# Keys of a local attention in one ring of blocks, and a stored order of instructions in place of a planner

## The chip, the cores and the metric

The kernel runs on one core of a Trainium2 chip. The metric is the time of one execution on the device in microseconds (us); the median of three runs of the kernel before is 1020.16 us (1020.14 to 1020.78). The engines are named as in the profile: PE (TensorE, with PEld for its weight loads), DVE (VectorE), ACT (ScalarE), POOL (GpSimd), and SP, the queue that issues every DMA here. Each engine is given its instructions in a fixed order, and they wait on semaphores of the other engines.

## The reference

Causal attention with a window of 64 positions over 4 batches, 8 heads, 576 positions and 64 channels, then two gated layers over the 2304 tokens (512 to 1536 to 512 channels):

```python
mask = (rel >= 0) & (rel < 64)
attn = softmax(where(mask, scale * q @ k.T, -1e9)); x = attn @ v
xn = x / sqrt(mean(x * x) + 1e-06) * rms_g
x = (silu(xn @ w_gate) * (xn @ w_val)) @ w_out          # first layer
x = (sigmoid(x @ w2_gate) * (x @ w2_val)) @ w2_out      # second layer
```

## The kernel before, in words

**Attention.** The work unit is 64 query positions of one batch with all heads; a batch has 9 units, 36 in all. Queries and keys are loaded in tiles of 128 positions, that is two units; the last tile of a batch holds one. With a window of 64, unit i needs the keys of its own 64 positions and of the 64 before. `st_s` computes its scores: four head pairs, for each a product of 128 query rows (two heads) with 128 keys in f32. In an odd unit both key blocks lie in one tile, and L387 is one matmul of 128 columns. In an even unit (other than the first of a batch) the blocks lie in two tiles, and L389 and L390 are two matmuls of 64 columns each. Keys lie in two buffers `kt` by turns, and the third tile of the program in a place of its own (`kt2`). The mask is added by a matmul (L383) in the first two blocks of tokens, and by DVE (L399) in the others; then follow the row maximum (L396 or L400), four exponentials on ACT (L403), and the division (L404 to L406). `st_tr` transposes on PE (L419), `st_pv` multiplies with the values (L455).

**The layers.** Tokens go in six blocks of 384. Float32 weights and activations are carried as pairs of f16 numbers, high and low part, and each product is three f16 matmuls. A gate or value product for 128 of the 1536 channels is twelve matmuls into one PSUM bank of two (`gv`, L551); there are 288 such products. ACT reads a gate product (L563), and then DVE reads it in the gate step L565 (first layer); DVE's L576 or L578 reads the value product. The bank is free for the next product only then. L592 to L597 split the result, and L611 to L613 (first layer) or L617 to L619 (second) multiply with the output weights.

**The weights** arrive in float64 bit patterns in 1 MB pieces, and `w_max` (L220), `w_conv` (L244 to L256) and `w_split` (L302 to L315) turn them into f16 pairs on DVE and ACT. This takes place beside attention, mostly in the first half of the program.

**The order.** The program is traced once. `arrange` then groups the instructions (a run of matmuls into one bank counts as one), gives each a length by the rules in `price`, finds from the tiles they touch which must wait for which, and lays them on the engines by eight rounds of list scheduling forward and backward. The best of these rounds gives the order on every engine, which is pinned with dependences that cost no semaphore.

## Time and profile before

| | us |
|---|---|
| median of three runs | 1020.16 |
| the profiled execution | 1016.32 |
| its span, first to last instruction | 1014.5 |
| PE busy in it | 959.0 |
| DVE busy in it | 584.4 |
| ACT busy in it | 409.7 |

The profile shows one execution, the profiled one; the runs took somewhat longer than it. A matmul in f32 appears as two records. Busy times of an engine are unions: what overlaps counts once. The end of a matmul in the profile is modelled, so what a group takes is best read from the start of one group to the start of the next.

### The profile page before, as it was taken

What the parts mean: (1) busy time and instruction counts of PE and PEld (TensorE: products, weight loads), DVE (VectorE), ACT (ScalarE), POOL (GpSimd) and SP (SyncE); (2) the same over time, 40 slices, a digit from 0 to 9 for tenths busy, and PEclk for the clock granted to TensorE, in tenths of its full rate; (3) what the DMA queues carried; (4) which work ended last, traced back from release to release, by engine and by line L of the source; (5) the groups of instructions that cost most, each with busy time, mean ns of one, the idle gap of its engine ahead of it and who ended that gap; (6) DMA issues with size and microseconds to landing.
All of it is one profiled execution on the core that took longest, in us unless ns stands there. A gap on an engine that the chain in (4) does not pass through costs nothing.

```text
span 1014.5 us, 14919 instructions
## 1 busy us (share of the span) xinstructions
PE 959.0 (95%) x6176; PEld 583.0 (57%) x6176; DVE 584.4 (58%) x1124; ACT 409.7 (40%) x787; POOL 34.9 (3%) x40
## 2 busy tenths in 40 slices
PE   6667899789999999999999999999999999999998
PEld 6535666456655675675555555555555555555554
DVE  6989998998778888978838813212222222222221
ACT  5478867567342446344414312222222222122122
POOL 0110000100010001001001000000000000000000
PEclk9789999999999999999999999999999999999999
DMA  8455345041530220220013000000000000000000
GB/s 294 122 178 166 116 126 177 11 162 31 197 120 1 52 85 21 95 94 12 1 42 115 12 1 1 1 1 32 1 32 1 1 32 1 1 32 1 1 32 31
DMA packets 43187, 61.54 MB, mean 61 GB/s; under 512 B 23408, under 2 KB 31984, under 8 KB 38640
## 3 DMA queue, kind: packets, MB, share of 16 engines
q1 hardware_dynamic: 43120, 60.60, 18.4%
q8 instruction: 48, 0.79, 0.3%
q14 instruction: 19, 0.16, 0.1%
HBM read 55.87 MB, written 4.72 MB: 60 GB/s over the span
## 4 chain that ended last, share of the span: by engine, by line
PE 80%; DVE 14%; ACT 4%; issue 1%; POOL 0%; DMA 0%; SPq 0%; ACTq 0%; POOLq 0%
PE gv L551 47%; PE o L619 5%; PE o L618 5%; PE o L617 5%; PE o L611 4%; PE o L612 4%; PE o L613 4%; PE at L455 1%; DVE wmax L220 1%; DVE wl L256 1%; DVE th L565 1%; DVE wl L315 1%; PE at L390 1%; PE at L419 1%; PE at L387 1%
## 5 line engine op out<-in xcount | busy, mean ns | idle before, releaser
L551 PE MATMUL gv<-xhl,wl 128*128 128x384 f16 x3456 | 600.8, 329 | 31.4 <-DVE th L565 27.7
L551 PEld LDWEIGHTS <-wl 128*128 128x128 f16 x3456 | 338.6, 98 | 268.3 <-issue 45.5
L597 DVE SCALAR_TENSOR_TENSOR hh<-th,hs,hh 128x384 f16<-128x384 f32 x72 | 44.5, 618 | 238.4 <-ACT hh L596 238.4
L596 ACT ACTIVATE hh<-th,hs 128x384 f16<-128x384 f32 x72 | 44.4, 616 | 256.0 <-PE o L618 243.5
L619 PE MATMUL o<-wl,hh 128*128 128x512 f16 x216 | 81.9, 379 | 0.0
L617 PE MATMUL o<-wl,hh 128*128 128x512 f16 x216 | 81.9, 379 | 0.0
L618 PE MATMUL o<-wl,hh 128*128 128x512 f16 x216 | 81.9, 379 | 0.0
L254 ACT ACTIVATE wl<-wl 128x1024 uint16<-128x1024 uint32 (+1 forms) x32 | 78.8, 2470 | 5.4 <-DVE wl L249 5.3
L578 DVE SCALAR_TENSOR_TENSOR th<-th,gv 128x384 f32<-128x384 f32 x72 | 39.9, 554 | 68.0 <-PE gv L551 68.0
L592 ACT ACTIVATE hh<-th 128x384 f16<-128x384 f32 x48 | 25.1, 523 | 122.8 <-PE o L613 101.4
L563 ACT ACTIVATE th<-gv,tg 128x384 f32<-128x384 f32 x72 | 41.8, 581 | 57.0 <-DVE hh L593 26.3
L611 PE MATMUL o<-hh,wl 128*128 128x384 f16 x192 | 62.8, 327 | 0.0
L612 PE MATMUL o<-hh,wl 128*128 128x384 f16 x192 | 62.7, 327 | 0.0
L613 PE MATMUL o<-hh,wl 128*128 128x384 f16 x192 | 62.6, 326 | 0.0
L563 ACT ACTIVATE th<-gv,be 128x384 f32<-128x384 f32 x72 | 41.8, 580 | 48.9 <-DVE hh L597 43.2
L565 DVE SCALAR_TENSOR_TENSOR th<-th,gv 128x384 f32<-128x384 f32 x72 | 39.7, 551 | 16.9 <-ACT th L563 15.9
L593 DVE TENSOR_TENSOR hh<-th,hh 128x384 f16<-128x384 f32 x48 | 29.6, 617 | 33.0 <-ACT hh L592 32.4
L403 ACT ACTIVATE sm<-sm,nm 128x128 f32<-128x128 f32 x96 | 37.4, 391 | 17.6 <-DVE nm L400 17.5
L220 DVE TENSOR_REDUCE wmax<-wl 128x1 f32<-128x1024 f32 (+1 forms) x37 | 43.5, 1182 | 1.7 <-DMA wl<-in_moe_w_val_dram 1.7
L576 DVE SCALAR_TENSOR_TENSOR th<-th,gv 128x384 f32<-128x384 f32 x72 | 39.4, 547 | 8.2 <-PE gv L551 7.9
L613 PEld LDWEIGHTS <-wl 128*128 128x128 f16 x288 | 28.2, 98 | 18.8 <-issue 0.2
L611 PEld LDWEIGHTS <-wl 128*128 128x128 f16 x288 | 28.3, 98 | 18.3 <-issue 0.2
(168 smaller groups left out, 1040.5 us busy)
## 6 DMA issues: line engine op xcount, KB each, us to landing
wl<-in_moe_w_gate_dram SPq DMA_DIRECT2D x12, 1024.0 KB, 4.8
wl<-in_moe_w_val_dram SPq DMA_DIRECT2D x12, 1024.0 KB, 5.4
wl<-in_moe_w_out_dram SPq DMA_DIRECT2D x11, 1024.0 KB, 4.9
vn<-in_v_dram SPq DMA_DIRECT2D x28, 256.0 KB, 2.8
kt<-in_k_dram SPq DMA_DIRECT2D x15, 256.0 KB, 3.7
qbd<-in_q_dram SPq DMA_DIRECT2D x30, 128.0 KB, 3.7
out_dram<-vn SPq DMA_DIRECT2D x12, 256.0 KB, 2.0
out_dram<-sm SPq DMA_DIRECT2D x6, 256.0 KB, 2.0
```

What stands on the lines that cost most here:

```text
L220: V.tensor_reduce(out=r1[:, i:i + 1], in_=wraw(layer, j + i)[:, :, 1].bitcast(F32), axis=AX.X, op=ALU.max, apply_absolute_value=True)
L254: A.activation(out=r, in_=lo, func=AF.Copy, scale=2.0 ** -29)
L551: T.matmul(pb[:, 0:n], lhsT=w_, rhs=x_, start=(c == 0), stop=(c == m - 1))
L563: A.activation(out=th[:, 0:n], in_=pg[:, 0:n], func=AF.Tanh, scale=sc)
L565: V.scalar_tensor_tensor(out=th[:, 0:n], in0=th[:, 0:n], scalar=1.0, in1=pg[:, 0:n], op0=ALU.add, op1=ALU.mult)
L597: V.scalar_tensor_tensor(out=h[:, 1, 0:n], in0=th[:, 0:n], scalar=sc, in1=h[:, 0, 0:n], op0=ALU.mult, op1=ALU.subtract)
L611: T.matmul(o[c][:, 0:n], lhsT=wh[:, cs], rhs=hi, start=st, stop=False)
L612: T.matmul(o[c][:, 0:n], lhsT=wh[:, cs], rhs=lo, start=False, stop=False)
L613: T.matmul(o[c][:, 0:n], lhsT=wl[:, cs], rhs=hi, start=False, stop=en)
L617: T.matmul(o[t], lhsT=h[:, 0, ts_], rhs=wh, start=st, stop=False)
L618: T.matmul(o[t], lhsT=h[:, 0, ts_], rhs=wl, start=False, stop=False)
L619: T.matmul(o[t], lhsT=h[:, 1, ts_], rhs=wh, start=False, stop=en)
```

## The change

**The ring.** Keys now lie in one tile `kring` of 16 blocks of 64 keys: two slots of eight blocks, and in a slot two blocks (first and second half of the tile) for each head pair. A block of one slot and one of the other, for the same pair, are a constant step apart, so the two operands of an even unit become one operand with a step, and L389 and L390 become one matmul of 128 columns. Where the newer tile is in the first slot, the blocks come in swapped order (`swapped`): the mask is then a rolled one and the values are loaded in two halves of 64 rows, exchanged. The two units that touch the third tile of the program stay as they were. In the first unit of a batch, DVE's mask and maximum and the exponentials take 64 columns instead of 128, and a memset fills the rest (only in the blocks without the mask matmul).

```diff
+    kring = cst.tile([P, 4 * NP, 64], F32, name="kring")
+    def kslot(ti):
+        return (ti - (ti > 2)) % 2
+    def whole(ti):
+        return ti not in (2, 3)
+    def swapped(u):
+        b, i = units[u]
+        ti = b * TPB + i // 2
+        return i % 2 == 0 and i > 0 and whole(ti) and kslot(ti) == 0
...
-        a = kt2 if ti == 2 else ap_.tile([P, NP, P], F32, tag="kt", name="kt", bufs=2)
+        a = kt2 if ti == 2 else kring[:, 2 * NP * kslot(ti):2 * NP * kslot(ti) + 2 * NP, :].rearrange("p (c h) x -> p c (h x)", c=NP)
...
+            elif whole(ti):
+                x = 2 * c if swapped(u) else 2 * c + 1
+                y = 2 * NP + (2 * c + 1 if swapped(u) else 2 * c)
+                T.matmul(pb[:, c * P:(c + 1) * P], lhsT=lhsT, rhs=kring[:, x:y + 1:y - x, :], start=first, stop=first or c == NP - 1)
             else:
                 T.matmul(pb[:, c * P:c * P + 64], lhsT=lhsT, rhs=kt[ti - 1][:, c, 64:128], start=first, stop=first)
                 T.matmul(pb[:, c * P + 64:(c + 1) * P], lhsT=lhsT, rhs=kt[ti][:, c, 0:64], start=first, stop=first or c == NP - 1)
...
+        if swapped(u):
+            SY.dma_start(out=a[0:64], in_=v[b, s0 + 64:s0 + 128, :])
+            SY.dma_start(out=a[64:128], in_=v[b, s0:s0 + 64, :])
...
+            m = 1 if i == 0 or swapped(u) else 0
+            w = 64 if i == 0 else P
+            if i == 0:
+                V.memset(s[:, :, 64:P], 0.0)
+            V.scalar_tensor_tensor(out=s[:, :, 0:w], in0=pv[:, :, 0:w], scalar=scale, in1=masks[:, m:m + 1, 0:w].to_broadcast([P, NP, w]), op0=ALU.mult, op1=ALU.min)
```

**The order.** `spans`, `price` and the scheduling in `arrange` are gone. `arrange` still groups the instructions, and then unpacks a stored table of positions, one for each group, and pins that order. The table is for all five engines.

```diff
+ORDER = (
+    'c-nPV31CxIy1xIp*-n!*P1>XzO<P*pri@w&QkJ&Eq81dGVNhTY@gd8DhbWe1a48IkqF}|cID@Y+BPjdGC{F|jc!MbLP$*@a7HTaNx}|%YG)Z&s'
...
+    d = zlib.decompress(base64.b85decode(ORDER))
+    n = len(d) // 2
+    seq = list(itertools.accumulate(struct.unpack(f"{n}h", bytes(x for y in zip(d[:n], d[n:]) for x in y))))
+    for k in seq:
+        for i in ops[k][1]:
+            if before is not None and before.engine == i.engine:
+                tc.add_manual_dep(i, before.name, mybir.DependencyInfo(mybir.DependencyClass.NoSync, mybir.DependencyReason.DATA), reason="order")
+            before = i
```

Three places show what moves. First the head of SP's queue before (`qbd0`, `qbd1` are query tiles, `const16` the masks of the mask matmul, `const32` the identity and DVE's masks):

```order
L345 DMA kt_0_101<-in_k_dram 128x4x128
L343 DMA qbd0_81<-in_q_dram 64x8x64 x2
L753 DMA wl2_74<-const16 128x384
L345 DMA kt_1_107<-in_k_dram 128x4x128
L343 DMA qbd1_82<-in_q_dram 64x8x64 x2
L754 DMA ident_75<-const32 128x128
L355 DMA wl2_74<-in_v_dram 128x512 x2
```

And the same head now:

```order
L218 DMA wl2_74<-in_moe_w_gate_dram 128x2048
L362 DMA kring_77<-in_k_dram 128x4x128
L787 DMA wl2_74<-const16 128x384
L218 DMA wl2_74<-in_moe_w_val_dram 128x2048
L360 DMA qbd0_82<-in_q_dram 64x8x64 x2
L218 DMA wl2_74<-in_moe_w_gate_dram 128x2048
L360 DMA qbd1_83<-in_q_dram 64x8x64
L218 DMA wl2_74<-in_moe_w_val_dram 128x2048
L362 DMA kring_77<-in_k_dram 128x4x128
L360 DMA qbd1_83<-in_q_dram 64x8x64
L788 DMA ident_75<-const32 128x128
```

Four weight pieces of 1 MB, which stood behind keys, queries and values of the first tiles, now stand between and ahead of them. Second the head of DVE's order behind its memsets, before (`nm` are row maxima, `su` row sums, `wl2` here holds the attention weights):

```order
L396 TENSOR_REDUCE nm_0_140<-o_0_134 128x4
L397 TENSOR_SCALAR nm_0_140<-nm_0_140 128x4
L396 TENSOR_REDUCE nm_1_157<-o_1_151 128x4
L397 TENSOR_SCALAR nm_1_157<-nm_1_157 128x4
L404 TENSOR_SCALAR su_0_143<-su_0_143 128x4
L405 RECIPROCAL su_0_143<-su_0_143 128x4
L396 TENSOR_REDUCE nm_2_184<-o_2_174 128x4
L406 TENSOR_TENSOR wl2_74<-wl2_74,su_0_143 128x512
```

And now (L224 is L220 of before, L248 is L244, L253 is L249, L256 is L252, L251 is L247, L425 is L396):

```order
L224 TENSOR_REDUCE wmax_0_396<-wl2_74 128x1
L248 TENSOR_SCALAR wl1_73<-wl2_74 128x1024
L253 TENSOR_SCALAR wl2_74<-wl2_74 128x1024
L256 TENSOR_SCALAR wl2_74<-wl2_74 128x1024
L251 TENSOR_SCALAR wl1_73<-wl1_73 128x1024
L248 TENSOR_SCALAR wl1_73<-wl2_74 128x1024
L224 TENSOR_REDUCE wmax_0_396<-wl2_74 128x1
L253 TENSOR_SCALAR wl2_74<-wl2_74 128x1024
L228 TENSOR_SCALAR amax_84<-amax_84 128x2
L425 TENSOR_REDUCE nm_0_139<-o_0_133 128x4
```

The conversion of the first weights has moved ahead of the first scores. Third a place on PE in the third block of tokens, before, where a unit within a tile and one across two tiles stand between two gate products (`at` are score banks, `kt_0` and `kt_1` the two key buffers):

```order
L506 MATMUL o_1_151<-xhl_2_617,wl2_74 128x128
L387 MATMUL at_0_195<-kt_1_107,qbd0_81 128x128 x4
L389 MATMUL at_1_228<-kt_1_107,qbd1_82 128x64
L390 MATMUL at_1_228<-kt_0_101,qbd1_82 128x64
...
L551 MATMUL gv_0_168<-xhl_1_337,wl1_73 128x384
```

And the first such unit of that block now (L416 is the merged matmul, L489 is L455 of before, L412 is L387, L585 is L551):

```order
L585 MATMUL gv_1_200<-xhl_1_332,wl1_73 128x384
L416 MATMUL at_1_223<-kring_77,qbd1_83 128x128 x4
L489 MATMUL at_0_190<-pT_0_461,vn_0_118 64x64 x8
L412 MATMUL at_1_223<-kring_77,qbd1_83 128x128 x4
L585 MATMUL gv_0_167<-xhl_2_607,wl1_73 128x384
```

Eight matmuls of 64 columns in one unit, of which the first two stand above, have become four of 128.

## Rows read from the trace of the kernel before

**Rows 1.** The page: busy time, and PE in 40 equal slices (tenths).
```profile
PE 959.0 (95%) x6176; PEld 583.0 (57%) x6176; DVE 584.4 (58%) x1124; ACT 409.7 (40%) x787; POOL 34.9 (3%) x40
PE   6667899789999999999999999999999999999998
```

**Rows 2.** Waits of PE: line, releaser, us in total, times, longest.
```profile
PE gv L551 <- DVE th L565: 27.7, 16, 5.6
PE gv L551 <- DVE th L576: 3.7, 2, 1.9
```

**Rows 3.** Timeline of PE: start, us, operation, count, idle time before and its releaser.
```profile
203.98 2.11 PE L551 MATMUL gv<-xhl,wl 128*128 128x384 f16 x12 [3.01 <-DVE th L565]
```

**Rows 4.** Waits of PE after 205 us.
```profile
PE gv L551 <- DVE th L565: 4.9, 4, 2.1
PE gv L551 <- DVE th L576: 1.7, 1, 1.7
```

**Rows 5.** Four stages: length; busy us of PE, PEld, DVE, ACT, POOL; clock, DMA, GB/s.
```profile
0.00:18.00 18.00, 10.59 (x67) 9.78 (x67) 8.90 (x25) 8.09 (x36) 0.19 (x4) 1.00 0.85 247
0.00:52.28 52.28, 34.66 (x279) 29.55 (x280) 41.32 (x108) 26.60 (x73) 6.42 (x7) 0.87 0.69 207
0.00:203.93 203.93, 158.96 (x1208) 111.88 (x1209) 181.39 (x395) 140.45 (x282) 15.38 (x18) 0.94 0.47 148
203.93:1014.50 810.57, 800.07 (x4968) 471.14 (x4967) 403.00 (x730) 269.20 (x505) 19.54 (x22) 1.00 0.12 39
```

**Rows 6.** Timeline of PE at 126 us, at 167 us and at 210 us.
```profile
126.17 1.06 PE L387 MATMUL at<-kt,qbd 128*128 128x128 f32 x8
127.07 0.33 PE L389 MATMUL at<-kt,qbd 128*128 128x64 f32 x2
127.24 0.39 PE L390 MATMUL at<-kt,qbd 128*128 128x64 f32 x2
...
128.80 4.06 PE L551 MATMUL gv<-xhl,wl 128*128 128x384 f16 x24
...
167.29 0.69 PE L455 MATMUL at<-pT,vn 128*64 128x64 f32 x16
167.91 0.66 PE L419 MATMUL at<-ident,sm 128*128 128x128 f32 x4
168.40 2.11 PE L551 MATMUL gv<-xhl,wl 128*128 128x384 f16 x12
...
209.78 0.33 PE L611 MATMUL o<-wl,wl 128*128 128x384 f16 x1
...
210.26 0.33 PE L611 MATMUL o<-wl,wl 128*128 128x384 f16 x1
```

**Rows 7.** PE's weight loads by line: shape, count, busy us, mean ns, idle before.
```profile
L389 PEld LDWEIGHTS at<-kt,qbd 128*128 128x128 f32 x88 | 13.8, 192 | 0.6
L387 PEld LDWEIGHTS at<-kt,qbd 128*128 128x128 f32 x104 | 13.0, 192 | 0.5
```

**Rows 8.** DVE's instructions by line and shape: count, busy us, mean ns, idle before.
```profile
L249 DVE TENSOR_SCALAR wl<-wl 128x1024 int32<-128x1024 int32 x35 | 24.1, 691 | 0.2
L315 DVE SCALAR_TENSOR_TENSOR wl<-wl,isc,wl 128x1024 f16<-128x1024 f32 x15 | 19.1, 1276 | 2.5 <-ACT wl L313 2.4
L399 DVE SCALAR_TENSOR_TENSOR sm<-at,masks 128x512 f32<-128x512 f32 x24 | 16.4, 686 | 5.5 <-PE at L390 3.1 <-PE at L419 1.5 <-PE at L387 0.7
L405 DVE RECIPROCAL su<-su 128x4 f32<-128x4 f32 x36 | 6.4, 177 | 1.0
L525 DVE TENSOR_TENSOR xf<-xf,xhl 128x1536 f32<-128x1536 f32 x4 | 7.0, 1750 | 0.0
L533 DVE SCALAR_TENSOR_TENSOR xhl<-xf,cg,xhl 128x384 f16<-128x384 f32 x16 | 9.4, 614 | 1.2 <-ACT xhl L532 1.1
```

**Rows 9.** DVE's first score, SP's first issue, and the gate weights' loads (us to landing).
```profile
8.48 0.69 DVE L396 TENSOR_REDUCE nm<-o 128x4 f32<-128x512 f32 x1 [4.06 <-PE o L387]
0.72 0.68 SPq L345 DMA_DIRECT2D kt<-in_k_dram  x1
wl<-in_moe_w_gate_dram SPq DMA_DIRECT2D x12, 1024.0 KB, 4.8
```

More of the change, by code (lines that the diff above doesn't have):

```diff
@@ L1 @@
-import bisect
-import heapq
+import base64
+import itertools
 import math
+import struct
+import zlib
 from contextlib import ExitStack
@@ L54, in tile @@
     def tile(self, shape, dt, name, tag=None, bufs=1):
-        if bufs == 1:
-            return self.pool.tile(shape, dt, tag=tag or name, name=name, bufs=1)
+        if tag is None:
+            return self.pool.tile(shape, dt, tag=name, name=name, bufs=1)
         l = self.asked.setdefault(tag, (bufs, []))[1]
@@ L354, in load_v @@
         a = abuf("vn", st)
-        SY.dma_start(out=a, in_=v[b, s0:s0 + 128, :])
+        if swapped(u):
+            SY.dma_start(out=a[0:64], in_=v[b, s0 + 64:s0 + 128, :])
+            SY.dma_start(out=a[64:128], in_=v[b, s0:s0 + 64, :])
+        else:
+            SY.dma_start(out=a, in_=v[b, s0:s0 + 128, :])
         vn[u] = a
@@ L381, in st_s @@
         if st:
-            T.matmul(pv, lhsT=identb, rhs=maskb[:, m:m + 1, :].to_broadcast([P, NP, P]), start=True, stop=False)
+            if swapped(u):
+                for e in range(2):
+                    T.matmul(pv[:, :, 64 * e:64 * e + 64], lhsT=identb, rhs=maskb[:, m:m + 1, 64 - 64 * e:128 - 64 * e].to_broadcast([P, NP, 64]), start=True, stop=False)
+            else:
+                T.matmul(pv, lhsT=identb, rhs=maskb[:, m:m + 1, :].to_broadcast([P, NP, P]), start=True, stop=False)
         for c in range(NP):
@@ L942, in arrange @@
 def arrange(nc, tc):
-    ops, tiles = [], {}
-    last = None
+    ops, last = [], None
     for i in nc.cur_bb.bb.instructions:
@@ L948, in arrange @@
             continue
-        o = [s for s in map(spans, i.outs) if s]
-        n = [s for s in map(spans, i.ins) if s]
-        occ, lat = price(e, i, o, n)
-        key = o[0][0].name if e == "PE" else None
-        if e == "PE" and last is not None and last[0] == (key, i.bass_priority - len(ops[last[1]]["ins"])):
-            k = last[1]
-        else:
-            k = len(ops)
-            ops.append(dict(e=ENGINES.index(e), ins=[], occ=0.0, lat=0.0, acc=[]))
-        g = ops[k]
-        g["ins"].append(i)
@@ L1022, in arrange @@
-    topo, todo = [k for k in range(N) if not P[k]], [len(p) for p in P]
-    for k in topo:
-        for m, _ in S[k]:
-            todo[m] -= 1
-            if not todo[m]:
-                topo.append(m)
-    assert len(topo) == N, "a circle"
-    tail = [0.0] * N
-    for k in reversed(topo):
-        tail[k] = max([tail[m] + d for m, d in S[k]], default=occ[k])
-    best = None
-    urgency = [float(k) for k in range(N)] if START == "trace" else [-x for x in tail]
-    log = []
-    for r in range(ROUNDS):
-        at, end = place(P, S, urgency, False)
-        log.append(round(end))
-        if best is None or end < best[0]:
-            best = (end, at)
-        back, e2 = place(S, P, [-(at[k] + occ[k]) for k in range(N)], True)
-        log.append(round(e2))
-        urgency = [e2 - back[k] - occ[k] for k in range(N)]
@@ L1043, in arrange @@
-    if VERBOSE:
-        print("arranged", N, log)
-    end, at = best
-    for e in range(len(ENGINES)):
-        before = None
-        for k in sorted((k for k in range(N) if E[k] == e), key=lambda k: (at[k], k)):
-            for i in ops[k]["ins"]:
-                if before is not None:
-                    tc.add_manual_dep(i, before.name, mybir.DependencyInfo(mybir.DependencyClass.NoSync, mybir.DependencyReason.DATA), reason="order")
-                before = i
-    return ops, at, P
-VERBOSE = False
@@ L1057 @@
-START = "tail"
+        key = i.outs[0].bass_ap.tensor.name if e == "PE" else None
+        if e != "PE" or last != (key, i.bass_priority - len(ops[-1][1])):
+            ops.append((e, []))
+            last = (key, i.bass_priority)
+        ops[-1][1].append(i)
+        if e != "PE":
+            last = None
+    d = zlib.decompress(base64.b85decode(ORDER))
+    n = len(d) // 2
+    assert n == len(ops)
+    seq = list(itertools.accumulate(struct.unpack(f"{n}h", bytes(x for y in zip(d[:n], d[n:]) for x in y))))
@@ L1060 @@
+    assert sorted(seq) == list(range(n)) and [ops[k][0] for k in seq] == sorted((e for e, _ in ops), key=ENGINES.index)
+    before = None
+    for k in seq:
[3 more added lines that the diff above has]
+            before = i
 _INS = ['q', 'k', 'v', 'moe_w_gate', 'moe_w_val', 'moe_w_out', 'moe_rms_g', 'moe2_w_gate', 'moe2_w_val', 'moe2_w_out']
```

152 lines of the change are left out of this document (43 added, 109 removed).

## The prediction

> **What bounds the kernel now.** I read the page first. TensorE (PE) is busy for 959.0 of 1014.5 us, and the slices show where the other 55 us are: in the first fifth, while from about 325 us on the engine is at nine tenths throughout [rows 1]. So anything taken out of PE's own work late in the program shortens the time one for one, and early in the program somebody else decides. The waits of PE name him: 27.7 us, half of its idle time, wait for VectorE's (DVE's) gate step L565, and 3.7 us for L576 [rows 2]. Both read the bank of a gate or value product, so PE cannot write the next product before them. The timeline puts the last long one of these at 203.98 us, after 3.01 us of standing [rows 3]; after 205 us only 6.6 us of such waits are left [rows 4]. The stage table then shows who is late in front of it: up to 203.93 us DVE is busy for 181.39 us and idle for only 22.5; behind it PE is busy 800 of 811 us [rows 5]. Hence a sum that I use throughout. The end is what DVE has to do ahead of that step, plus what DVE idles until then, plus what PE has to do behind it, plus what PE loses behind it: 181.4 + 22.5 + 810.6 = 1014.5. The step is the 24th of its line. It frees the bank for the 47th of the 288 products of twelve L551 matmuls, and I follow that product into the new order.
>
> **The merged matmuls.** A unit of four head pairs in one tile (L387, four 128-column matmuls) runs from 126.17 to 127.07, 0.90 us; a unit across two tiles (L389 and L390, eight 64-column matmuls) from 127.07 to 128.80, 1.73 us [rows 6]. A half is therefore no cheaper than a whole. The weight loads say why: a half brings a load of 128x128, 192 ns, and so does a whole [rows 7]. The trace calls each f32 matmul twice, so a half is two records there. Of 16 units across two tiles, 14 become whole (the two that touch the third tile stay): 14 x 0.83 = 11.6 us of PE work. Each has the cover of DVE if it lies ahead of the 47th product. What stands behind that product, by the two orders: 8 units of halves before, 7 whole ones now (the other 7 stand ahead of it), so 8 x 1.73 - 7 x 0.90 = 7.5 us less. The new order has further moved one unit of transposes and value products (0.62 + 0.49 us) and seven triples of L611 to L613 (0.48 us each, 209.78 to 210.26) to the front of it [rows 6]: 4.5 us less. PE ahead of the product is the same to 0.1 us by these lengths. **PE behind: -12.0 us.**
>
> The Trainium skill has a rule against this term. "TensorE: Matmul & The Clock Gate", section Back-to-back issue gap, gives about 60 cycles up to 64 columns and 134 for 128, so two halves would cost less than one whole. The trace disagrees, with 1.73 against 0.90 us for the same columns; the section adds that the spacing of a stream of load and matmul is set by both, and that is the half that these rows bear out. By the rule alone the 7.5 us would not come and the time would be 1013 or 1014 instead of 1006; the first rival below has it as a mechanism of this kernel.
>
> **The order on DVE.** Ahead of the step that frees the bank for the 47th product the new table has these differences: one more of L315 (1.28); seven more of about 0.69 each (two L399, two L400, one L406, one copy of L302, and one more of L247 and L249 together); four more small ones of L404 and L405 at 0.18; one fewer of L525 (1.75) and of L533 (0.61) [rows 8]. 1.28 + 4.83 + 0.72 - 2.36 = 4.5. One L399 and one L400 of these are only half as wide, since they belong to a first unit of a batch, less about 0.7 together by halving the row, and a memset of 256 elements comes with them, which no row shows at that size; I let it cost 0.2. **DVE ahead: +4.0 us.** That the net is small hides a large move: ahead of the first gate step there are 25 us more than before, nine L220 instead of four, seven L256 instead of three, six L315 instead of two. The first gate step itself thus comes later, near 41.3 + 25 + 8 idle = 74 us instead of 52.28 [rows 5]; it is work brought forward, and the +4.0 is what is left of it at the step that counts.
>
> **DVE's idle time until then.** 22.5 us now, of which 11.0 stand ahead of 52.28 us and 9.1 ahead of 18 us [rows 5]: it waits 4.06 us for the first scores at 8.48, and then for each of the next [rows 9]. The new order begins DVE with weight work and puts the gate weights first on SP's queue. A load of 1 MB lands 4.8 us after its issue, the first issue stands at 0.72 us [rows 9], so DVE can start at about 5.6 rather than 8.5, and eight large weight instructions (some 7 us) stand ahead of the first score. What is pushed back is keys and queries: with all that the first scores need, 2.7 MB stand in the new queue, at the 247 GB/s of the first 18 us [rows 5] 11 us after the first issue, near 12, about when DVE is through with those eight. The identity, which the transposes need, lies behind some 5.3 MB, 21 us; ScalarE's (ACT's) exponentials come later too. Queued behind them on PE are transposes, value products and the next scores, and PE has time there. The bounds are 12 us (what is idle now after 52.28 us, 11.5, and almost none ahead) and 31 us (all of the present, and 8 of new waiting). I take 18.5: the wait for the first scores and part of those for the next go, the rest stays. **-4 us.**
>
> **PE's loss behind the 47th product.** Nothing to all of the 6.6 us of waits [rows 4] may go. Counted over both orders with the lengths of the rows, the sum of DVE ahead and PE behind falls alike, to 14 us under its peak by the 65th product, so the room there is the same as now; only another order of the steps in between can save something, and I take a third. **-2 us.** PE's clock of 0.87 up to 52 us [rows 5] costs nothing in either order as long as DVE is late there; the new one is emptier in front, and a slow start of the first products has some 6 us of cover, by which their sum lies under the peak.
>
> Small edits: the eight 64-wide exponentials lie on ACT, which is busy 140 of 204 us [rows 5]; six more value loads (halves of 64 rows) sit on a queue that waits for buffers; the ring has the same two slots that the two buffers had. All of them cost nothing while these covers last, and less than 1 us otherwise.
>
> **The sum.** 1014.5 - 12.0 + 4.0 - 4 - 2 = 1000.5 us of span, 14.0 less. The profiled execution took 1016.32 us, 1.8 more than its span, and would take 1002.3. The median of the runs shown, 1020.16, stands 3.8 above that execution, so the runs should give **1006 us**. The bounds of idle time and waits give 995 to 1020; counting DVE's work ahead by lengths of rows comes out 4 us above the 181.4 that the trace has, which is the error of such a count.
>
> **Rivals.**
> - *The merge saves nothing.* The operand is now two pieces of the ring, 64 keys apart from one another or more, and could be fed as slowly as two matmuls. For it: no strided f32 operand of this kind is in the rows. Against: it is the load that costs, and there is one per matmul [rows 7]. Then 7 x 0.83 = 5.8 us of the term return: 1012. It still would be faster, through the order. Chance 0.07.
> - *The new front idles DVE.* In its order DVE stands in front of scores, exponentials and rms steps that come later than now because 4 MB of weights lead on the queue. Without my two gains the sum is 1006.5 of span; from 8 us more idle time than now (30.5 up to the 47th product) the kernel is slower than before. With 15 more, 1021.5 of span and 1027 us. For it: the first gate step is 22 us later, and the sum of DVE ahead and PE behind lies within 1 us of its peak from the 27th to the 47th product, so no wait in that stretch is covered. Against: some 25 us of independent weight work stand between the attention steps there. Chance 0.09.
> - *The order gives back what the merge gains*, by waits for ACT, whose exponentials share its queue with the conversions of the weights: 12 + 2 us of them at a place where nothing covers them, 1020. Chance 0.05.
> - *The table removes nearly all idle time*: DVE idle for 3 us up to the 47th product (19.5 less than now) and no waits behind it (6.6 less): 1014.5 - 8.0 - 26.1 = 980.4 of span, 986 us. It would need every hand-off between four engines to be met. Chance 0.06.
> - The forecast itself, with idle time and waits between the bounds: 989 to 1016, chance 0.73.
>
> The range 989 to 1016 holds the forecast and the first rival, 0.80; its low end is the lower bound less the error of the count. A difference of 0.2%, 2 us, is what can be told from none. Faster: 0.73 + 0.07 + 0.06 = 0.86; same 0.05; slower 0.09.
>
> **What the new profile would show.** A unit from two tiles lasts 0.9 us, and PE's busy time falls by about 12 us. If the unit lasts 1.7, the first rival. DVE's first weight instruction near 5.6 us, its first gate step near 75, its busy time to the release of the 47th product near 185 us and its idle time near 18; above 30, the second. Waits of PE for L565 (its line is then 599) behind that product near 4 us. The forecast is wrong if PE's busy time falls and the span does not, for then the order has lost it again in front of the 47th product.

## The result, and the profile after

The changed kernel takes **985.33 us** (median; 984.43 to 985.55) against 1020.25 us of the kernel before on the same chip (1020.14 to 1020.78): ratio 0.9655, 95% interval 0.9638 to 0.9672, so 35 us faster. The forecast was 14 us faster (1006), and 985 lies below its range. The profiled execution took 985.49 us with a span of 983.7, 30.8 less than the span before.

The page, as in [rows 1]: PE does 10.6 us less, and its slices are full from the fourth on, at about 75 us, where before they were full only from the tenth, at about 230. What is new is the front: three slices of 4, 6 and 7.

```profile
PE 948.4 (96%) x6064; PEld 577.8 (59%) x6064; DVE 575.2 (58%) x1126; ACT 405.4 (41%) x787; POOL 32.6 (3%) x40
PE   4679999999999999999999999999999999999998
DVE  8999999998888988978578431211211221122221
```

The waits of PE (line, releaser, us in total, times, longest) answer to [rows 2]. The gate step, now L599, held PE up for 27.7 us; 1.8 are left. What PE waits for now are transfers and the first results, nearly all of it ahead of the first product at 69 us (3.8 us are left behind that).

```profile
PE o L408 <- DMA wl<-const: 7.0, 1, 7.0
PE o L412 <- DMA qbd<-in_q_dram: 3.7, 1, 3.7
PE gv L585 <- DVE th L599: 1.8, 4, 0.9
```

Four stages (length; busy us of PE, PEld, DVE, ACT and POOL; clock, DMA share, GB/s) answer to [rows 5]: the first 18 us, up to the first gate step, up to the release of the 47th product, and from that product to the end.

```profile
0.00:18.00 18.00, 5.21 (x19) 3.89 (x19) 13.26 (x24) 5.42 (x7) 1.05 (x5) 1.00 0.97 308
0.00:73.58 73.58, 46.33 (x317) 38.57 (x318) 65.13 (x153) 52.32 (x109) 5.64 (x9) 0.79 0.69 210
0.00:192.59 192.59, 163.66 (x1203) 117.35 (x1204) 179.07 (x406) 144.93 (x298) 13.35 (x18) 0.91 0.52 163
193.69:983.70 790.01, 783.62 (x4857) 459.81 (x4854) 394.98 (x720) 259.40 (x490) 19.22 (x22) 1.00 0.12 38
```

Read with the frame of the prediction: DVE busy 179.1 us ahead of the release (181.4 before), DVE idle 192.6 - 179.1 = 13.5 (22.5 before), 1.1 us from the release to the product, and 790.0 us behind it (810.6 before). So 10.3 us of the 30.8 come ahead of the 47th product and 20.5 behind it.

The merged unit, by the timeline of PE (start, us), answers to [rows 6]: the next instruction starts 0.89 us behind it. Of the weight loads of [rows 7] there are half as many for it, each as long as before.

```profile
84.78 1.05 PE L416 MATMUL o<-kring,qbd 128*128 128x128 f32 x8
85.67 0.65 PE L585 MATMUL gv<-xhl,wl 128*128 128x384 f16 x3
```
```profile
L416 PEld LDWEIGHTS at<-kring,qbd 128*128 128x128 f32 x88 | 11.1, 192 | 0.5
```

DVE's first weight step and its first gate step, by its timeline (before: 8.48 us for its first score [rows 9]; 52.28 [rows 5]):

```profile
5.76 1.22 DVE L224 TENSOR_REDUCE wmax<-wl 128x1 f32<-128x1024 f32 x1 [1.31 <-DMA wl<-in_moe_w_gate_dram]
```
```profile
73.03 0.55 DVE L599 SCALAR_TENSOR_TENSOR th<-th,gv 128x384 f32<-128x384 f32 x1
```

### The profile page after: what moved, and what is told of

It reads as the page before. It is cut to its first block, busy times and chain, and to the rows that moved or that the text cites. A ratio compares the mean times of both kernels' runs of the same rounds, so it can differ in the third digit from the quotient of the medians.

```text
span 983.7 us, 14773 instructions
## 1 busy us (share of the span) xinstructions
PE 948.4 (96%) x6064; PEld 577.8 (59%) x6064; DVE 575.2 (58%) x1126; ACT 405.4 (41%) x787; POOL 32.6 (3%) x40
## 4 chain that ended last, share of the span: by engine, by line
PE 87%; DVE 9%; ACT 2%; DMA 1%; issue 0%; SPq 0%; POOL 0%; ACTq 0%; DVEq 0%
PE gv L585 54%; PE o L652 5%; PE o L653 5%; PE o L651 5%; PE o L645 5%; PE o L647 5%; PE o L646 5%; PE at L489 1%; PE at L412 1%; DVE wl L260 1%; DVE wmax L224 1%; ACT wl L258 1%; DMA qbd<-in_q_dram 1%; PE at L453 1%; DVE wl L253 1%; PE at L416 1%
## 5 line engine op out<-in xcount | busy, mean ns | idle before, releaser
L585 PE MATMUL gv<-xhl,wl 128*128 128x384 f16 x3456 | 591.3, 327 | 2.8 <-DVE th L599 1.8
L585 PEld LDWEIGHTS <-wl 128*128 128x128 f16 x3456 | 337.8, 98 | 232.7 <-issue 6.5
L258 ACT ACTIVATE wl<-wl 128x1024 uint16<-128x1024 uint32 (+1 forms) x32 | 78.6, 2472 | 11.5 <-DVE wl L253 11.3
L599 DVE SCALAR_TENSOR_TENSOR th<-th,gv 128x384 f32<-128x384 f32 x72 | 39.7, 551 | 18.9 <-ACT th L597 18.5
L626 ACT ACTIVATE hh<-th 128x384 f16<-128x384 f32 x48 | 24.9, 521 | 62.4 <-DVE th L610 37.1
L224 DVE TENSOR_REDUCE wmax<-wl 128x1 f32<-128x1024 f32 (+1 forms) x37 | 43.7, 1184 | 1.9 <-DMA wl<-in_moe_w_gate_dram 1.3
L437 ACT ACTIVATE sm<-sm,nm 128x128 f32<-128x128 f32 (+1 forms) x96 | 36.9, 386 | 18.9 <-DVE nm L434 18.8
L647 PEld LDWEIGHTS <-wl 128*128 128x128 f16 x288 | 28.2, 98 | 18.6
L646 PEld LDWEIGHTS <-wl 128*128 128x128 f16 x288 | 28.2, 98 | 17.9 <-issue 0.8
L645 PEld LDWEIGHTS <-wl 128*128 128x128 f16 x288 | 28.2, 98 | 17.4
```

The lines of the kernel that those rows point to most:

```text
L224: V.tensor_reduce(out=r1[:, i:i + 1], in_=wraw(layer, j + i)[:, :, 1].bitcast(F32), axis=AX.X, op=ALU.max, apply_absolute_value=True)
L258: A.activation(out=r, in_=lo, func=AF.Copy, scale=2.0 ** -29)
L585: T.matmul(pb[:, 0:n], lhsT=w_, rhs=x_, start=(c == 0), stop=(c == m - 1))
L645: T.matmul(o[c][:, 0:n], lhsT=wh[:, cs], rhs=hi, start=st, stop=False)
L646: T.matmul(o[c][:, 0:n], lhsT=wh[:, cs], rhs=lo, start=False, stop=False)
L647: T.matmul(o[c][:, 0:n], lhsT=wl[:, cs], rhs=hi, start=False, stop=en)
```

## The experiments

Each run stood beside runs of the kernel before on the same chip (medians 1018 to 1020 us); ratios are to those. The times of before spread by 4 us from execution to execution (1016.0 to 1020.7), those of the changed kernel by 1, so effects against the changed kernel are given by the medians of the times and by the spans; by the ratios they differ by up to 3 us. Theory A at the start: in the changed kernel PE waits for nobody behind its first product, so PE's work behind it counts in full and VectorE's only ahead of it. Theory B: the frame of the prediction, where the release of the 47th product decides and work of PE ahead of it has cover.

### Merge and order apart

*e1_halves*: the changed kernel, its order kept, with each merged product as two of 64 columns again.

```diff
-                T.matmul(pb[:, c * P:(c + 1) * P], lhsT=lhsT, rhs=kring[:, x:y + 1:y - x, :], start=first, stop=first or c == NP - 1)
+                T.matmul(pb[:, c * P:c * P + 64], lhsT=lhsT, rhs=kring[:, x, :], start=first, stop=first)
+                T.matmul(pb[:, c * P + 64:(c + 1) * P], lhsT=lhsT, rhs=kring[:, y, :], start=first, stop=first or c == NP - 1)
```

> The changed kernel, its table and its ring, but each merged matmul again as two of 64 columns. Theory A (in the changed kernel PE waits for nobody behind its first product at 69 us, so every us of PE work behind it counts): 13 of the 14 units lie there, 13 x 0.83 = 10.8 us, 985.3 + 10.8 = 996. Theory B (the frame of the prediction: VectorE's release of the 47th product sets the end, and PE work ahead of it is covered): only 7 units count, 5.8 us, 991. If halves cost half of a whole: 985.

Measured 997.03 us (ratio 0.9801, 0.9766 to 0.9837): 11.7 us more, 11.3 by the spans. A holds, B falls. The stages say where: up to the release, and from the 47th product on, they are 5.6 us longer each (198.18 against 192.59, 795.58 against 790.01). Ahead of the release DVE's busy time is the same, 179.4 us, and its idle time rises from 13.5 to 18.7. A unit of PE there has no cover: DVE waits for PE as PE waits for DVE.

```profile
0.00:198.18 198.18, 167.77 (x1258) 122.75 (x1259) 179.44 (x406) 145.24 (x298) 13.35 (x18) 0.91 0.51 159
199.42:995.00 795.58, 789.42 (x4913) 465.86 (x4910) 395.14 (x720) 259.47 (x490) 19.23 (x22) 1.00 0.12 38
```

*e2_planner*, *e3_planner_pool*: merged products, the order found by the planner of before. The change also lets a single-buffer tile with a tag keep one name, so that the planner sees its reuse; e2 has the old rule, e3 the new one (the lines below).

```diff
-        if bufs == 1:
-            return self.pool.tile(shape, dt, tag=tag or name, name=name, bufs=1)
+        if tag is None:
+            return self.pool.tile(shape, dt, tag=name, name=name, bufs=1)
```

> The ring and the merged matmuls with the planner of the kernel before in place of the table. Theory A: the planner's order keeps its waits up to 204 us, so only units behind them save, 7 to 8 times 0.83: 1020.2 - 6 = 1014. Rival (the merge, not the table, made the change large): below 1000.

> As the kernel with the planner and the merge, with the changed kernel's rule for buffers too: a tile with one buffer keeps its name, so that the planner sees that two users of the transposed weights or of the block of tokens share it. Theory A: 1014, as without. Rival (the planner was blind to these two buffers, and its waits come from that): most of the 35 us, about 990 to 1000.

Measured 1010.42 (0.9916, 0.9893 to 0.9938) and 1005.62 us (0.9872, 0.9849 to 0.9895); both lie between their two forecasts. By the ratios the merge gives 8.6 us under the planner, 13 with the naming rule; so it is not the large part. Some of it may be a truer plan: `price` gives an f32 matmul of 64 columns 112 ns and one of 128 columns 218, where [rows 6] have about 220 for either, and no run tells this apart. From e3 to the changed kernel 20 us are left for the table (22 by the ratios): by the traces 8.1 up to the start of the 47th product (201.79 against 193.69 us) and 12.3 behind it (802.3 against 790.0).

### Where in the program the table gains

*e8_table_first*, *e9_planner_first*: two orders in one kernel, cut at VectorE's 45th gate or value step, which releases the 47th product: the table up to there and the planner behind, or the reverse.

```diff
+    one, two = (tab, pln) if FIRST == "table" else (pln, tab)      # e8: "table", e9: "planner"
...
+        head = one[e][:upto[e]]                                    # up to the 45th step and what it needs
+        s = set(head)
+        order.append(head + [k for k in two[e] if k not in s])
```

> The merged kernel; the table's order up to VectorE's step that frees the bank for the 47th product (45 gate and value steps) and for all that this needs on the other engines, the planner's order for the rest. Theory A, by parts: what the table wins in front (10 us at the 47th product) stays, the 6.6 us of waits behind it come back: 985.3 + 6.6 = 992. Rival (all is won in front, the rest of the order does not matter): 985.

> The merged score products, with the order of the planner until VectorE's 45th gate or value step (up to the release of the 47th product), and the table's order behind it. Theory A (in the changed kernel TensorE waits for nobody behind its first product, so that all the gain of the order is in how VectorE and TensorE are filled ahead of the 47th product): the planner and merge together measured 1005.6 us, the table behind the 47th product was worth 9 us (994.2 against 985.3), so the rest of the 20 us, 11 us, belongs to the front and is lost here: 996 to 997 us, with waits of TensorE ahead of the 47th product. Rival (the gain lies behind, in the order of the products' steps): 985 to 989 us.

Measured 994.22 (0.9765, 0.9745 to 0.9785) and 1003.19 us (0.9851, 0.9832 to 0.9870). The first is near A's 992. The second is 18 us above the changed kernel, not the 11 expected by subtraction. Behind the 47th product it is the changed kernel (790.67 against 790.01), and that product starts 19.1 us later. Some 8 of these are the planner's front, as in e3: VectorE's 45th step ends at 201.50 us, with VectorE busy for 181.5 us and idle for 20.0. The other 11 us are the seam of the two orders: TensorE's row goes over to the table's, which has seven triples ahead of the 46th product, and the first of them waits 9.0 us for ScalarE's weight conversion L319, whose input VectorE makes only behind its 45th step. So e9 does not price a front by itself.

```profile
0.00:201.50 201.50, 155.40 (x1148) 108.38 (x1148) 181.47 (x399) 140.84 (x289) 16.45 (x18) 0.90 0.47 148
203.39 0.50 PE L647 MATMUL o<-wl,wl 128*128 128x384 f16 x1 [8.96 <-ACT wl L319]
212.83:1003.50 790.67, 783.70 (x4859) 458.95 (x4855) 393.00 (x718) 258.67 (x486) 19.21 (x22) 1.00 0.12 38
```

### How tight VectorE's row is

Four reduces that nobody reads (expected 4.6 us, 4.97 on the trace) at row 100, 250, 700 or 1000 of VectorE in the changed kernel, and at row 640 (the same time, 374 us) of the planner's finished order in the kernel before.

```diff
+        for _ in range(4):
+            V.tensor_reduce(out=mhalf, in_=ident.unsqueeze(1).to_broadcast([P, 8, P]), axis=AX.XY, op=ALU.max)
...
+    ops.append(("DVE", extra))
+    seq.insert(d[100], len(ops) - 1)        # e4; e5: 250, e10: 700, e13: 1000
...
+            l.insert(640, extra)            # e11, in the kernel before
```

> The changed kernel with four VectorE reduces of 128x1024 that nobody reads, some 4.6 us in all, at VectorE's 100th row (about 50 us, ahead of the first gate product at 69 us). Theory A: VectorE's work ahead of the first product sets when TensorE's row of products begins, and nothing is waited for behind it, so the whole 4.6 us comes out: 990 us. Rival (VectorE's idle time of 8 us ahead of its first gate step covers it): 985 to 986 us.

> The same four reduces (4.6 us) at VectorE's 250th row, some 125 us into the run, between the first and the 47th product, where VectorE is busy for 119.6 of 124.7 us. Theory A, with VectorE also the bound of this stretch: its slack ahead of the 47th product's release is 1.1 us, so 3 to 4.6 us come out: 988 to 990 us. Rival (TensorE alone is the bound there, since it waits for nobody): 985 to 986 us.

> The same four reduces (4.6 us) at VectorE's 700th row, some 374 us into the run, where VectorE is busy for 88 of 100 us and TensorE for all of it. Theory A (VectorE decides only until its steps run ahead of TensorE): nothing comes out, 985 to 986 us. Rival (VectorE's steps release TensorE's products over the whole run, so that any work added to it comes out): 989 to 990 us.

Measured 990.29 (0.9727, 0.9711 to 0.9742), 989.54 (0.9719, 0.9702 to 0.9735) and 989.82 us (0.9724, 0.9708 to 0.9741). The first two fit, with the first product of e4 at 73.61 instead of 69.00 us. The third refutes A: VectorE's work still counts in full at 374 us (by the trace the products are 1.4 us early ahead of it, a matter of the front, and 4.3 us late behind it, 5.6 in all). The timeline of PE in e10 shows what had no slack: a triple and a product right behind the VectorE results that they read.

```profile
385.72 0.32 PE L646 MATMUL o<-hh,wl 128*128 128x384 f16 x1 [3.09 <-DVE hh L627]
...
386.92 0.48 PE L585 MATMUL gv<-xhl,wl 128*128 128x384 f16 x1 [0.71 <-DVE th L599]
```

So theory C: it is the table that leaves no slack.

> The kernel before with four VectorE reduces of 128x1024 that nobody reads (4.6 us in all) put into its finished order at VectorE's 640th row, some 374 us into the run, where the same work cost the changed kernel all of its 4.6 us. Theory C (what leaves no slack at 374 us is the table: a product of TensorE stands right behind the VectorE result that it reads): in the planner's order VectorE's row there has gaps of about 1 us that nothing waits for, so 0 to 1.5 us come out and the ratio to before is 1.000 to 1.0015. Rival (VectorE's steps release TensorE's products in any order of this kernel): 4.6 us, ratio 1.0045.

> The changed kernel with the same four reduces (4.6 us) at VectorE's 1000th row, beyond 600 us, where VectorE is busy for about 20 of 100 us. Theory C says that slack is what decides: the gate and value steps of the first layer are over there, so 0 to 1 us comes out, 985 to 986.5 us. Rival (the table sets every reader right behind its VectorE result to the end): 989 to 990 us.

Measured 1023.18 us for e11 (ratio 1.0052, 1.0033 to 1.0071) and 985.40 for e13 (0.9673, 0.9652 to 0.9693). C falls too: the planner's order loses most of it as well. By its trace the products run 2.65 us late until then, from the front, and 6.57 behind: 3.9 us were lost here, 3.0 of them in one wait of PE, the row below. Lack of slack is a property of both orders, and it ends between 374 us and 627, where e13's reduces stand.

```profile
PE at L419 <- DVE sm L406: 3.0, 1, 3.0
```

### The front by its inputs

*e6_loads_late*: the first four weight loads behind the twelve other loads on SyncE's queue. *e12_dve_less*: the maxima of four weights over 128 columns instead of 1024.

```diff
+    w = [k for k in sp[:16] if "moe_w" in str(ops[k][1][0].ins[0].bass_ap.tensor.name)][:4]      # e6
+    rest = [k for k in sp if k not in w]
+    seq = [k for k in seq if ops[k][0] != "SP"] + rest[:12] + w + rest[12:]
...
-            V.tensor_reduce(out=r1[:, i:i + 1], in_=wraw(layer, j + i)[:, :, 1].bitcast(F32), ...)
+            e = 128 if layer == 0 and 4 <= j + i < 8 else None                      # e12
+            V.tensor_reduce(out=r1[:, i:i + 1], in_=wraw(layer, j + i)[:, 0:e, 1].bitcast(F32), ...)
```

> The changed kernel with the first four weight loads issued behind the twelve other loads at the head of SyncE's queue. The prediction counted the earlier first weight as one reason why VectorE idles less ahead of the 47th product. If that is so, VectorE's first weight step starts 6 to 7 us later than 5.76 us, and 4 to 6 us of its 8.5 us of idle time cannot absorb it, since the row is tight: 989 to 991 us. Rival (the first 12 us of VectorE's work are not what the first product waits for, since score work fills them): 985 to 986 us.

> The changed kernel, its order as it is, with the maximum of four weights (the fifth to eighth of the first layer, reduced between 37 and 58 us) taken over 128 of their 1024 columns only: VectorE has about 4 x 1.0 us less ahead of the first product, and the scale of these weights is then not the reference's. Theory C (VectorE's and TensorE's rows are both tight, so a us of VectorE's work ahead of the first product is a us of the time): 981 to 982 us. Rival (VectorE waits longer for its partners instead, TensorE, ScalarE and transfers being as late as it): 984 to 986 us.

Measured 994.54 (0.9763, 0.9742 to 0.9784) and 983.85 us (0.9659, 0.9638 to 0.9680). In e6 VectorE's first weight step comes 9.9 us later, at 15.69, the first product 9.3 us later and the end 9.2: nearly all of it passes through, more than either expectation. In e12 the four maxima take 0.28 instead of 1.21 us, 3.7 less in all, but the first product comes only 2.1 us earlier, and the span is 2.2 shorter: a value between the two, and one that the ratio (0.9655 for the changed kernel) does not tell from nothing. Of what VectorE gains it idles 1.3 us more ahead of the release, so not all that it needs from other engines comes earlier by as much. Below are its first weight step in e6, and the four maxima of e12 of full and of short length.

```profile
15.69 1.22 DVE L224 TENSOR_REDUCE wmax<-wl 128x1 f32<-128x1024 f32 x1 [11.25 <-DMA wl<-in_moe_w_gate_dram]
```
```profile
L225 DVE TENSOR_REDUCE wmax<-wl 128x1 f32<-128x1024 f32 x4 | 4.8, 1212 | 1.3 <-DMA wl<-in_moe_w_gate_dram 1.3
L225 DVE TENSOR_REDUCE wmax<-wl 128x1 f32<-128x128 f32 x4 | 1.1, 280 | 0.0
```

### Which engine's row it is

In each, the planner (as in e3) plans everything with the rows of one engine or more held as the table has them: SyncE (e14), VectorE (e15), TensorE (e16), SyncE and TensorE (e18), these two and VectorE (e19).

```diff
+    for e in HELD:                       # ("SP",), ("DVE",), ("PE",), ("SP", "PE"), ("SP", "PE", "DVE")
+        l = [k for k in seq if E[k] == ENGINES.index(e)]
+        for j, k in zip(l, l[1:]):
+            P[k].append((j, occ[j]))
```

> Merged products and the planner, which is given SyncE's queue as the table has it (weights first) and orders the other engines itself. Planner and merge alone: 1005.6 us; the table: 985.3. Theory V (what the table gains lies in VectorE's row, and the loads only serve it): the planner keeps its own VectorE row, 1002 to 1007 us. Rival S (the early weights are the gain, as delaying them by 10 us cost 9.2 us): 993 to 997 us.

> The same with VectorE's row as the table has it, the other engines' rows by the planner. Theory V: the planner has to serve that row with the loads and products in the order in which it needs them, so most of the gain comes, 986 to 991 us. Rival P (TensorE's row is the gain): 998 to 1005 us.

> The same with TensorE's row as the table has it, the other engines' rows by the planner. Theory V: VectorE's row is then the planner's own answer to TensorE's row, and only part of the gain comes, 993 to 1000 us. Rival P: 985 to 990 us.

> Merged products and the planner, with SyncE's and TensorE's rows as the table has them; VectorE's, ScalarE's and GpSimd's rows by the planner. If the gains add up (SyncE's row saved VectorE 4.5 us of idle time ahead of the 47th product, 20.2 to 15.8; TensorE's row saved 8.6 us behind it, 802.3 to 793.7), the planner's 1005.6 us falls by 6.0 and 7.7: 990 to 993 us. Rival (the rows only pay together with VectorE's): 995 to 1000 us. Third (these two rows are the whole gain): 985 to 987 us.

> The same with VectorE's row held too; only ScalarE's and GpSimd's rows are the planner's. If these two engines have slack (ScalarE is busy 41% of the time), the whole gain is there: 985 to 987 us. Rival (ScalarE's row, on which VectorE's weight steps wait, matters): 989 us or more.

| held | us | ratio, interval | DVE busy | DVE idle | behind the 47th |
|---|---|---|---|---|---|
| none (e3) | 1005.62 | 0.9872, 0.9849 to 0.9895 | 181.5 | 20.2 | 802.3 |
| VectorE (e15) | 1005.36 | 0.9866, 0.9841 to 0.9890 | 179.3 | 24.9 | 802.9 |
| SyncE (e14) | 999.59 | 0.9804, 0.9784 to 0.9823 | 181.2 | 15.8 | 799.4 |
| TensorE (e16) | 997.92 | 0.9785, 0.9768 to 0.9801 | 179.5 | 22.9 | 793.7 |
| SyncE, TensorE (e18) | 991.77 | 0.9735, 0.9707 to 0.9763 | 181.4 | 16.7 | 793.3 |
| these and VectorE (e19) | 989.80 | 0.9711, 0.9681 to 0.9741 | 179.1 | 15.6 | 790.3 |
| all (the changed kernel) | 985.33 | 0.9655, 0.9638 to 0.9672 | 179.1 | 13.5 | 790.0 |

The last three columns are the stages up to the release and behind the product, in the profiled execution (in e15 the longest of its runs, 1009.0 us); of e3, e14, e15 and e16:

```profile
0.00:201.74 201.74, 155.37 (x1160) 107.25 (x1161) 181.52 (x399) 141.37 (x290) 16.45 (x18) 0.93 0.48 149
201.79:1004.10 802.31, 793.35 (x4904) 464.03 (x4903) 402.65 (x728) 267.04 (x497) 20.12 (x22) 1.00 0.12 39
```
```profile
0.00:196.92 196.92, 157.50 (x1160) 109.96 (x1161) 181.16 (x397) 139.07 (x282) 9.76 (x18) 0.90 0.47 150
```
```profile
0.00:204.22 204.22, 165.07 (x1194) 117.43 (x1195) 179.29 (x406) 144.57 (x297) 12.92 (x18) 0.87 0.49 154
```
```profile
203.35:997.00 793.65, 783.96 (x4856) 459.69 (x4854) 400.79 (x728) 266.22 (x493) 22.27 (x22) 1.00 0.11 38
```

My theory that VectorE's row carries the gain falls, though its forecast for e16 (993 to 1000) came true: held alone that row is worth nothing; its busy time falls to the table's 179.3 us, and its idle time rises to 24.9, waiting for rows that were planned otherwise. e14 lies between its two forecasts. SyncE's early weight loads take 4.5 us of idle time out of the front; TensorE's row takes 8.6 us out of the part behind it. The two add up as forecast in e18. VectorE's row on top of them takes 3.0 us out of the part behind it (793.3 to 790.3), though the intervals of e18 and e19 overlap. In e19 ScalarE's and GpSimd's rows alone are the planner's; its interval reaches from 988 to 994 us by the ratio, and the changed kernel's ends at 987, so these rows are worth something, from about 1 us up, but how much was not settled.

### Three steps moved into gaps

*e17_gaps*: three steps of VectorE's row, ahead of the first product, put into its idle gaps.

```diff
+    d = [k for k in seq if ops[k][0] == "DVE"]
+    for a, b in ((21, 18), (91, 87), (144, 140)):
+        d.insert(b, d.pop(a))
```

> The changed kernel with three moves in VectorE's row ahead of the first product: a sign mask (L251, 0.6 us) into the gap of 1.4 us at 14 us, a packing step (L260, 1.1 us) into the gap of 1.6 us at 45 us, an addition (L253, 0.6 us) into the gap of 1.5 us at 65 us. If VectorE's row is the bound up to the first product at 69 us, 2.3 us of its work now lie in gaps and the first product comes 1 to 2.3 us earlier: 983 to 984.4 us. Rival (the chains through ScalarE and TensorE end just behind VectorE's): 985 to 985.5 us.

Measured 983.66 us (982.83 to 984.31; ratio 0.9648, 0.9634 to 0.9662). The gap that a packing step went into, in the changed kernel (first fence) and in this one:

```profile
44.85 0.21 DVE L234 TENSOR_SCALAR tg<-pw,pgam 128x1 f32<-128x1 f32 x1
46.70 0.69 DVE L425 TENSOR_REDUCE nm<-o 128x4 f32<-128x512 f32 x1 [1.64 <-PE o L419]
```
```profile
44.84 1.22 DVE L260 CUSTOM_DVE_ANT_0 wl<-wl,wl 128x2048 uint16<-128x2048 uint16 x1
46.56 0.69 DVE L425 TENSOR_REDUCE nm<-o 128x4 f32<-128x512 f32 x1 [0.51 <-PE o L419]
```

The time is inside the expected range and the lowest of all kernels here, 1.7 us below the changed kernel by the medians, and its runs lie apart from the latter's (984.43 to 985.55). But the two ran on different occasions, the intervals of their ratios overlap, and the profile hardly supports it: the first product comes 0.6 us earlier, not 1 to 2.3, and the profiles of e5, e10 and e13, with the table's rows up to there, have it at 68.71 to 69.94 us. That the moves make the kernel faster is possible, and not shown.

## Why the prediction was wrong

Its direction, its main bound and the frame held, and so did several steps by their size: the first weight step at 5.76 us (forecast 5.6), the first gate step ending at 73.6 (near 74), the unit of 0.89 us (0.90). PE's work behind the product fell by 12.3 us (12.0), from the start of one matmul to the start of the next: 7.6 through the merge (7.5) and 4.7 through what was moved ahead (4.5). The table of isolated gaps in the Trainium skill ("TensorE: Matmul & The Clock Gate", Back-to-back issue gap) has two halves cheaper than one whole. These f32 products disagree: in e1 the same columns in halves cost 11.7 us more. The prediction's rival at 986 us has the time by luck and not the mechanism: it wanted DVE idle for 3 us and 13.5 were measured. Three readings in the prediction are wrong and carry nothing: PE's slices are full from about 230 us, not 325; by its own lengths PE's work ahead of the product grows by 0.4 us and is not the same to 0.1; and 995 less the error of the count is 991, not 989.

Three terms were mis-sized in the same direction, and a small one in the other, 17 us of span together:

1. **The cover for merged units ahead of the 47th product** ("each has the cover of DVE"). There is none. Taking these units apart again moved the release by 5.6 us, 5.2 of it as idle time of DVE (e1). Most of the -9.0 us of idle time against my -4 is this, in the table's order (in the planner's, e3, idle time falls by 2.3 only); the rest, 3.8, is about what I gave the order. That early loads matter there is shown by e14 (4.5 us) and e6 (9.3 us for 9.9 of delay).
2. **DVE ahead of the release**: +4.0 forecast, -2.3 measured. The count by lines found L315 (+1.0) and the pair L525, L533 (-2.2) rightly, and the memset that it let cost 0.2 without a row took 0.3. It gave 4.1 us for the seven steps of about 0.69 us where 2.7 came, +0.7 for the small steps L404 and L405 where 1.2 went away, and it priced steps of one line and shape alike in both orders (the steps that read products are 45 in both, one L565 fewer and one L576 more). But L593, 21 times in both, takes 2.05 us less, 1.5 of it in a single one that lasts 2.05 us instead of 0.55 in the trace of before, beside an all-reduce of GpSimd (last section). And the steps of at most four elements are as many (146 before, 150 after) but 2.7 us shorter together: from the start of one to the start of the next, idle time left out, they take 0.10 us, but 0.15 before and 0.13 after where the next one reads the result, as 66 do before and 30 after.
3. **PE's loss behind the product**: I let a third of 6.6 us go. Listed waits fell from 6.7 to 2.5. Another 4.0 us show in no wait: without listed waits the part behind the product takes 803.8 us before and 787.5 after, 16.3 less, of which 12.3 are PE's work. In the trace of before 23 products start some 0.13 us late behind a triple of the first layer (3.1 us; in that of after five behind triples of the second, 0.8), as in the rows below: the matmul before starts at 314.13, one every 0.16 us, so the next was due at 314.29; it starts at 314.43, just behind the VectorE step that frees its bank (313.82 + 0.55). The profile counts no idle time, since the last matmul's modelled end covers it. About 1.6 are ten matmuls of 0.32 us at the lower clock level, 1.2 GHz (granted clock 0.61 from 300.5 to 304 us), behind a wait of 2.07 us. That wait and one of 2.08 at 476.79 us, the two longest, each follow an L593 that lasts 2.02 us instead of 0.56, again beside the all-reduce. To hold TensorE's row is enough for the part that no wait shows: in e16, with VectorE's row planned anew around it, PE is busy for 784.0 us behind the product instead of 793.4 (e3), of which 5.3 is work moved ahead. The listed waits stay (5.0 us in e3, 5.8 in e16, 5.4 in e18) and go only with VectorE's row held too (2.7 in e19).
4. The release now comes 1.1 us ahead of its product (0 forecast), which takes 1.1 us back.

```profile
314.13 0.33 PE L613 MATMUL o<-hh,wl 128*128 128x384 f16 x1
314.43 0.81 PE L551 MATMUL gv<-xhl,wl 128*128 128x384 f16 x4
```
```profile
313.82 0.55 DVE L565 SCALAR_TENSOR_TENSOR th<-th,gv 128x384 f32<-128x384 f32 x1
```
```profile
300.50:304.00 3.50, 3.21 (x12) 1.64 (x12) 3.29 (x9) 0.00 (x0) 0.00 (x0) 0.61 0.00 0
```

The misses add up: the forecast of 1000.5 us of span, less 6.3 (DVE ahead), less 5.0 (idle time), less 6.2 (loss behind: 4.2 + 4.0 against 2), less 0.3 (PE's work, 12.3 instead of 12.0), plus 1.1, is 983.8; the span is 983.7. The other 3.8 us are no mechanism of the change. The forecast added them because the three runs of before stand that much above its profiled execution, and those of after don't. They go with the granted clock: beside the experiments the kernel before takes about 1016.3 us at up to 0.988, 1018.7 at 0.981 and 1020.3 at 0.978, and the profiled execution had 0.987. One profile is uncertain by as much: in e11, which has the order of before up to 374 us, the same front was 2.6 us later than in the profile shown.

The step under the first three is one: I took "VectorE sets the pace up to the 47th product, TensorE behind it" as two engines with one owner for each stretch, so that work of the other is free there. Where the rows of four engines hand over every few microseconds, a stretch in which DVE is busy 89% and PE 78% has no owner; PE's work ahead (e1), the loads (e6) and DVE's work (e4, e5) each came out nearly in full, while work taken from DVE paid only in part (e12).

What stays open: how much ScalarE's and GpSimd's rows are worth (e19), what the steps beside the all-reduce cost in the end, and whether e17 gains.

## What to carry to other kernels

Before work is costed at nothing because another engine is "the bound" of its stretch, look at that engine's idle time there: if it waits for the engine whose work changes, there is no cover, and a few reduces that nobody reads, put in at several places, measure the slack for the price of one run each. A new order is worth more than the waits in the table of waits: starts that are late by a tenth of a microsecond, and matmuls at the lower clock behind a wait, show only when the same instructions are summed by line in both traces. So do single steps that last longer than their like: list the longest of each line, and see what ran beside them. Which part of an order earns its gain can be found by holding one engine's row and planning the rest anew.

## What the runs showed of the hardware

The clock fell without any wait of TensorE that the profile counts. In the profile of the changed kernel the 24 matmuls of two products behind a run of one-column matmuls take 5.74 us instead of 4.06, with a granted clock of 0.80 from 120 to 125 us, between the levels of 1.2 and 2.4 GHz. In e17 (second fence) the same instructions of TensorE in the same order run at 2.4 GHz, the granted clock being 1.00 from 115 to 130 us.

```profile
119.71 2.73 PE L531 MATMUL o<-wl,xhl 128*128 128x1 f32 x24
122.30 5.74 PE L585 MATMUL gv<-xhl,wl 128*128 128x384 f16 x24
```
```profile
119.54 2.73 PE L531 MATMUL o<-wl,xhl 128*128 128x1 f32 x24
122.13 4.06 PE L585 MATMUL gv<-xhl,wl 128*128 128x384 f16 x24
```

So the same row of TensorE differs from execution to execution by 1.7 us at such a place, and most of the profiles here have a stretch of lower clock somewhere between 70 and 200 us. Differences under 2 us between single profiles in that part were not read as effects.

A 64-column f32 product costs as much as one of 128 columns: halves cost 11.7 us more over 14 units, 0.84 us each (0.83 by [rows 6]), and the operand of two pieces of the ring is read as fast as one piece. VectorE's steps of at most four elements cost 0.15 us in the old row where the next step reads their result and 0.10 where it doesn't.

Some steps of VectorE last longer beside GpSimd. In the trace of before three L593 last 2.02 to 2.05 us, where the other L593 take about 0.55, and each starts within 0.4 us behind the start of an all-reduce (L487) of GpSimd and runs beside it. The first stands ahead of the release; behind the other two ScalarE's and VectorE's next gate step come late, and TensorE waits.

```profile
180.89 2.52 POOL L487 PARTITION_ALL_REDUCE xhl<-xhl  x1 [6.16 <-DVE pw L225]
180.92 2.05 DVE L593 TENSOR_TENSOR wl<-th,wl 128x384 f16<-128x384 f32 x1
```
```profile
297.19 2.78 POOL L487 PARTITION_ALL_REDUCE xhl<-xhl  x1 [9.78 <-DVE xhl L486]
297.51 2.02 DVE L593 TENSOR_TENSOR hh<-th,hh 128x384 f16<-128x384 f32 x1
300.79 0.99 PE L551 MATMUL gv<-xhl,wl 128*128 128x384 f16 x4 [2.07 <-DVE th L565]
```

In all twenty traces every VectorE step that lasts over 0.3 us longer than is usual for its line and shape runs beside such an all-reduce, but not every step beside one is longer: L599 at 181.37 us in the changed kernel takes its usual 0.55. In the changed kernel no L593 (now L627) is longer; two other steps are, at 414 and 416 us, and TensorE waits 0.9 us behind them. From these rows I estimate that 4 to 5 us of the 30.8 lie here (1.9 ahead of the release, up to 1.5 in each of the two waits). No run moves the all-reduce alone, so that share is not shown.
